# The first load of wq moved ahead of the critical section and cut into 16 and 112 partitions, the store's wait moved into a section of its own, and the order of waits turned round

## The chip, the core and the metric

The kernel runs on one core of one Trainium2 chip. Its time is the device time of one execution in microseconds (us), taken as the median of several runs; lower is better. A profile comes from one more execution, in which every instruction and every DMA packet is recorded. The span in it reaches from the first to the last recorded instruction and is a little shorter than the execution's device time.

## The reference

One token `x` of 576 values is normalised (mean and variance, epsilon 1e-5, no scale or offset) to `xn`. Two branches read `xn`, and the result is their sum with `x`:

```python
q = (xn @ wq)                                   # 576 -> 32 heads x 128
p = softmax(q . k_cache * 128**-0.5)            # k_cache: 32 heads x 16384 keys x 128
A = (p . v_cache) @ wo                          # v_cache likewise; wo: 4096 -> 576
B = (gelu(xn @ w_gate) * (xn @ w_up)) @ w_down  # 576 -> 4608 -> 576, tanh form of gelu
out = x + A + B
```

All of it is float32. One head's keys are 8 MB and its values another 8 MB, so 32 heads read 537 MB; the five weight matrices add some 51 MB.

## The kernel before

The order of all work is written out by hand; there is no planner. The class `Order` (L40 to L114) keeps, for every buffer, a log of who last wrote or read which part, with the semaphore and value that says when. `needs` (L59) turns the operands of a new instruction into a list of (semaphore, value) pairs, in the order in which the log gives them: what the operands read comes first, then what the destination overwrites. `op` (L87) issues compute instructions and `dma` (L103) transfers. Both put the first pair of the list on the instruction itself and a separate wait instruction ahead of it for each of the others. L106 is such a separate wait of a transfer, L107 the transfer itself.

The function `tile_decode_kernel` opens one critical section (L120) and calls `decode` in it. At its entry SP releases the other engines, at its exit all five meet. Everything below happens inside.

Three slots of 64 KB per partition over all 128 partitions hold what is streamed from memory: `slot_a`, `slot_b` and `slot_v` (in the code `sa`, `sb`, `sv`). Nearly all transfers are issued by SP, in the order of the program:

1. L197 loads the first 512 rows of `wq` into `slot_a`: four rows of the matrix on each partition, 16,384 values or 64 KB in one piece, 128 partitions, 8 MB. L198 loads the last 64 rows of `wq` into `slot_b`. Then parts of `w_gate` and `w_up` go into `slot_v` and into the rest of `slot_b`. The three small loads of `x` are issued by ACT.
2. Meanwhile VectorE (DVE) and ScalarE (ACT) normalise `x`; TensorE (PE) spreads it over the partitions; DVE writes the copies that the projections use into `z`. `project` (L245) multiplies with `wq` (called at L258: first the part in `slot_b`, then the four quarters in `slot_a`) and later with `w_gate` and `w_up` in `ffn`.
3. The heads. Keys of head h go to `slot_b` (even h) or `slot_a` (odd h), the values of the head before to `slot_v` (L340, L342). DVE multiplies the whole 128 x 16384 slot of keys by the query and reduces it to 128 x 128 scores (both L185); then come the maximum over partitions by way of PE and DVE (L355, L357), its scaled negative `nb` on ACT, the exponentials `pe` on ACT, and 32 products with the values on PE (L305, a loop in PE's own instructions). The next keys for a slot are issued when DVE has reduced the old ones, the next values when PE has used the old ones.
4. The end: `w_down` and `wo` are loaded, DVE sums 28 rows of `w_down`, PE does the rest, DVE copies the result of 4 x 144 values into `z`, SP stores it (L432), and SP waits for the store to land (L433). The section's exit follows, and then the program's own meeting of engines (L457).

Of the kernel before, what the change touches and what calls it, by code (L numbers as in the profile page):

```python
# [8 lines left out]
F32 = mybir.dt.float32  # L9
# [4 lines left out]
P = 128  # L14
H, SK, DH = 32, 16384, 128
D, DF = 576, 4608
R = SK // P
SUB = 64
DJ = 4
DM = P * DJ  # L20
# [15 lines left out]
SLOT_AT = 27904  # L36
SLOT_B = R * DH * 4


class Order:  # L40
# [46 lines left out]
    def op(self, eng, emit, out, *ins, also=(), signal=None):  # L87
        reads, writes = [a for a in ins if a is not None], [out, *also]
        need = self.needs(eng, reads, writes)
        for sem, value in need[1:]:  # L90
            getattr(self.nc, eng).wait_ge(sem, value)
        i = emit(getattr(self.nc, eng))
        if need:
            i._wait_ge(*need[0])
        value = self.count[eng] + 1
        if signal is None:
            self.count[eng] = value
            i.then_inc(self.sem[eng], 1)
        else:
            i.then_inc(signal, 1)  # L100
        self.note(eng, self.sem[eng], value, reads, writes)

    def dma(self, dst, src, sem, value=16, eng="sync", out=False):  # L103
        need = self.needs(eng, [src] if out else [], [] if out else [dst])
        for s, v in need[1:]:
            getattr(self.nc, eng).wait_ge(s, v)  # L106
        i = getattr(self.nc, eng).dma_start(dst, src)  # L107
        if need:
            i._wait_ge(*need[0])
        i.then_inc(sem, 16)  # L110
        if value and not out:
            self.note("dma", sem, value, [], [dst])


SIZES = {}


@with_exitstack
def kernel(ctx: ExitStack, tc: tile.TileContext, x, k_cache, v_cache, wq, wo, wg, wu, wd, out):
    with tc.tile_critical():  # L120
        decode(tc, x, k_cache, v_cache, wq, wo, wg, wu, wd, out)


def decode(tc, x, k_cache, v_cache, wq, wo, wg, wu, wd, out):
    nc = tc.nc
    o = Order(tc)
    names = iter(range(1000))

    def sem():
        return tc.alloc_semaphore(f"d{next(names)}")  # L130

    def sbuf(name, *shape):
        n = 1
        for s in shape[1:]:
            n *= s
        t = nc.alloc_sbuf_tensor(name, [P, n], F32)
        SIZES[t.name] = n
        return t.ap()[: shape[0]]
# [3 lines left out]
        SIZES[t.name] = 512 * banks  # L142
        return t.ap()

    def slot(name, i):
        t = nc.alloc_sbuf_tensor_at(name, [P, R * DH], F32, offset=SLOT_AT + i * SLOT_B)
        SIZES[t.name] = R * DH
        return t.ap()

    kv = k_cache.rearrange("b h (p n) d -> (b h) p (n d)", p=P)  # L150
    vv = v_cache.rearrange("b h (p n) d -> (b h) p (n d)", p=P)
    xf = x.rearrange("b s d -> (b s) d")
# [1 line left out]
    wmain = {n: w[:DM].rearrange("(p j) f -> p (j f)", j=DJ) for n, w in (("q", wq), ("g", wg), ("u", wu))}  # L154
    wtail = {n: w[DM:].rearrange("d (s f) -> (d s) f", s=2) for n, w in (("q", wq), ("g", wg), ("u", wu))}
    wov = wo.rearrange("(p t) f -> p (t f)", t=WO_T)
    wdv = wd.rearrange("(p t) f -> p (t f)", t=WD_T)

    sa, sb, sv = slot("slot_a", 0), slot("slot_b", 1), slot("slot_v", 2)
    ident, ones = sbuf("ident", P, P), sbuf("ones", P, P)  # L160
    eps_t, par, same, quarter = sbuf("eps_t", P, 1), sbuf("par", P, 2), sbuf("same", P, 32), sbuf("quarter", P, 4)
    x2 = sbuf("x2", P, HALF)
# [21 lines left out]
    def dve(name, out, *ins, **kw):  # L184
        o.op("vector", lambda e: getattr(e, name)(out, *ins, **kw), out, *[a for a in ins if isinstance(a, bass.AP)],  # L185
             *[a for a in kw.values() if isinstance(a, bass.AP)])
# [5 lines left out]
    def load(dst, src, **kw):  # L192
        o.dma(dst, src, sem(), **kw)
        return dst

    ROW3 = 3 * DF
    load(sa, wmain["q"])  # L197
    qt = load(sb[:, ROW3 : ROW3 + QS], wtail["q"])  # L198
    row3, tails, at = {}, {}, 0
    for n in "gu":  # L200
# [132 lines left out]
    for h in range(H):  # L333
        s = h % 2
# [32 lines left out]
    def load_rows(t, at, src, lo, n):  # L367
        load(t[:, at * D : (at + n) * D], src[:, lo * D : (lo + n) * D])
        return [t[:, (at + j) * D : (at + j + 1) * D] for j in range(n)]

    first = load_rows(sb, 0, wdv, 0, WD_A)
# [7 lines left out]
    wo_rows, lo = [], 0  # L379
# [36 lines left out]
    for j, w in enumerate(wo_rows):  # L416
# [4 lines left out]
        if j == WO_T - 4:  # L421
            dve("tensor_add", x2[:64], x2[:64], pairs[1][64:, :HALF])
            dve("tensor_add", x2[:64], x2[:64], pairs[0][:64, :HALF])
            for i, g in enumerate(quart):
                r, lo = 32 * (i // 2), i % 2 * QUART
# [2 lines left out]

    o4 = z[:, P : P + QUART]
    dve("tensor_copy", o4, acc4)  # L430
    s_out = sem()
    o.dma(of.rearrange("o (a f) -> (o a) f", a=4), o4[0:P:32, :], s_out, eng="sync", out=True)  # L432
    nc.sync.wait_ge(s_out, 16)  # L433


# [26 lines left out]
```

## Time and profile before

| what | value |
|---|---|
| runs of the kernel before | 1364.62 us median of 3 (1364.61 to 1365.01) |
| device time of the profiled execution | 1364.62 us |
| its span, first to last instruction | 1362.8 us |
| time outside the span | 1.82 us |
| TensorE clock granted, mean | 0.629 of full speed |

How to read the profile: PE is TensorE's matmul and PEld its weight load, DVE VectorE, ACT ScalarE, POOL GpSimd, SP the engine that issues transfers, SPq its queue. A line of a timeline gives start, duration, engine, program line and operation, and in brackets how long the engine had been idle before and what released it. A view by windows gives the busy time of every engine in a stretch, then the clock of PE, the mean busy share of the core's 16 DMA engines (a packet counts in the stretch in which it begins, so short stretches can show more than 1) and what they moved in GB/s. A transfer is cut into packets, and a packet is done by one DMA engine. The chain of work is followed back from the last instruction to what released it at each step.

### The profile page before, as it was taken

The numbers are of one execution on the slowest core, as the hardware profiler recorded it, in microseconds if no ns is written. First come the engines' busy times: TensorE is split into PE (matmuls) and PEld (weight loads), VectorE is DVE, ScalarE is ACT, GpSimd is POOL, SyncE is SP. The second block draws the span as 40 slices with busy tenths as digits, with TensorE's granted clock in tenths as the row PEclk, the third lists the DMA queues.
The fourth block names the chain that finished last, engine by engine and source line by source line (L and its number), as shares of the span: only waits on it lengthen the run. The fifth ranks groups of instructions, "written<-read, shape, count | busy, mean of one in ns | idle before, by whom it ended". The sixth has DMA issues, their size and how long they took to land.

```text
span 1362.8 us, 6967 instructions
## 1 busy us (share of the span) xinstructions
PE 446.2 (33%) x3012; PEld 161.7 (12%) x3012; DVE 1158.1 (85%) x195; ACT 63.2 (5%) x231; POOL 1.0 (0%) x7
## 2 busy tenths in 40 slices
PE   3431233333322333323223333323223333232237
PEld 1110111110111111101101111101111111011012
DVE  1069999899888888899888888998888888988882
ACT  0000000000000000000000000000000000000000
POOL 0000000000000000000000000000000000000000
PEclk9665666666556666666556666665566666655667
DMA  9999999999999999999999999999999999999998
GB/s 398 449 424 431 437 442 439 429 433 433 433 433 431 435 439 442 431 433 431 433 435 431 435 435 442 433 433 433 433 435 431 431 437 440 437 431 433 432 434 347
DMA packets 11832, 587.73 MB, mean 431 GB/s; under 512 B 1319, under 2 KB 1325, under 8 KB 1710
## 3 DMA queue, kind: packets, MB, share of 16 engines
q1 hardware_dynamic: 11816, 587.60, 99.6%
q8 instruction: 5, 0.08, 0.0%
q14 instruction: 5, 0.04, 0.0%
q10 hardware_dynamic: 6, 0.00, 0.0%
HBM read 587.60 MB, written 0.00 MB: 431 GB/s over the span
## 4 chain that ended last, share of the span: by engine, by line
DMA 49%; DVE 39%; issue 0%; PE 0%
DMA slot_b<-in_A_k_cache_dram 43%; DVE slot_b L185 20%; DVE scores L185 19%; DMA slot_b<-in_B_w_down_dram 3%; DMA slot_b<-in_A_wo_dram 3%; PE pg L182 0%; PE pg L317 0%; DVE z L185 0%; DVE nm L357 0%
## 5 line engine op out<-in xcount | busy, mean ns | idle before, releaser
L305 PE MATMUL po<-slot_v,pe 128*4 128x512 f32 x2048 | 293.0, 736 | 607.0 <-PEq L309 607.0
L185 DVE TENSOR_TENSOR slot_a<-slot_a,qs 128x16384 f32<-128x16384 f32 x16 | 275.6, 17223 | 42.7 <-DMA slot_a<-in_A_k_cache_dram 42.7
L185 DVE TENSOR_TENSOR slot_b<-slot_b,qs 128x16384 f32<-128x16384 f32 (+1 forms) x17 | 275.7, 16218 | 38.6 <-DMA slot_b<-in_A_k_cache_dram 38.6
L185 DVE TENSOR_REDUCE scores<-slot_b 128x128 f32<-128x16384 f32 (+1 forms) x17 | 275.7, 16216 | 0.6
L185 DVE TENSOR_REDUCE scores<-slot_a 128x128 f32<-128x16384 f32 x16 | 275.5, 17220 | 0.6
L305 PEld LDWEIGHTS po<-slot_v,pe 128*4 128x4 f32 x2048 | 56.6, 98 | 816.3 <-issue 816.3
L317 PE MATMUL pg<-ident,pm 128*1 128x128 f32 x32 | 11.9, 372 | 240.3 <-PEq L309 240.3
L185 DVE TENSOR_TENSOR slot_v<-pg,same 128x396 f32<-128x396 f32 (+1 forms) x6 | 3.4, 558 | 70.1 <-PE pg L182 69.8
L190 ACT ACTIVATE z<-po 128x512 f32<-128x512 f32 x33 | 19.7, 596 | 888.8 <-PE po L305 888.8
L305 PE MATMUL pc<-same,z 128*128 128x1 f32 x256 | 59.8, 355 | 0.0
L305 PEld LDWEIGHTS pc<-same,z 128*128 128x128 f32 x256 | 57.1, 328 | 0.5
L317 PEld LDWEIGHTS pg<-ident,pm 128*1 128x1 f32 x32 | 2.5, 79 | 245.5 <-issue 245.5
L357 DVE TENSOR_REDUCE nm<-pg 1x1 f32<-1x128 f32 x32 | 8.9, 279 | 17.8 <-PE pg L317 17.8
L185 DVE SCALAR_TENSOR_TENSOR slot_b<-slot_b,hT 128x576 f32<-128x576 f32 x27 | 22.1, 819 | 0.9
L305 PE MATMUL pg<-nm,ones 1*128 1x1 f32 x64 | 17.7, 343 | 14.8 <-PEq L309 14.8
L305 PEld LDWEIGHTS pg<-nm,ones 1*128 1x128 f32 x64 | 15.9, 306 | 24.2 <-issue 24.2
L190 ACT ACTIVATE nb<-pg 128x1 f32<-128x1 f32 x32 | 5.5, 171 | 235.7 <-PE pg L305 235.7
L305 PE MATMUL pqs<-qcur,ones 1*128 1x128 f32 x64 | 15.4, 321 | 1.4 <-PEq L309 1.4
L182 PE MATMUL pg<-slot_b,z 128*32 128x396 f32 (+1 forms) x72 | 7.7, 594 | 19.1 <-DMA slot_b<-in_B_w_gate_dram 19.1
L190 ACT ACTIVATE pe<-scores,nb 128x128 f32<-128x128 f32 x32 | 12.8, 401 | 2.9
L305 PEld LDWEIGHTS pqs<-qcur,ones 1*128 1x128 f32 x64 | 9.4, 182 | 28.7 <-issue 28.7
L185 DVE TENSOR_TENSOR x<-x,qb 64x288 f32<-64x288 f32 x2 | 0.9, 452 | 11.5 <-PE qb L182 11.4
(75 smaller groups left out, 123.6 us busy)
## 6 DMA issues: line engine op xcount, KB each, us to landing
slot_b<-in_A_k_cache_dram SPq DMA_DIRECT2D x2, 4096.0 KB, 23.9
slot_b<-in_B_w_down_dram SPq DMA_DIRECT2D x1, 8064.0 KB, 42.6
slot_b<-in_B_w_gate_dram SPq DMA_DIRECT2D x1, 6912.0 KB, 55.5
slot_a<-in_B_w_up_dram SPq DMA_DIRECT2D x1, 6912.0 KB, 39.8
slot_a<-in_A_wo_dram SPq DMA_DIRECT2D x1, 3456.0 KB, 41.3
slot_v<-in_B_w_gate_dram SPq DMA_DIRECT2D x1, 2304.0 KB, 29.0
slot_v<-in_B_w_up_dram SPq DMA_DIRECT2D x1, 2304.0 KB, 37.5
slot_a<-in_B_w_down_dram SPq DMA_DIRECT2D x1, 2304.0 KB, 28.5
```

What stands on the lines that cost most here:

```text
L182: o.op("tensor", lambda e: e.matmul(outp, lhsT, rhs, start=start, stop=stop), outp, lhsT, rhs, signal=signal)
L185: o.op("vector", lambda e: getattr(e, name)(out, *ins, **kw), out, *[a for a in ins if isinstance(a, bass.AP)], *[a for a in kw.values() i ...
L190: o.op("scalar", lambda e: e.activation(out, src, func, **kw), out, src, kw.get("bias") if isinstance(kw.get("bias"), bass.AP) else None, ...
L305: i = nc.tensor.matmul(dst, lhs, rhs, start=start, stop=stop)
L317: nc.tensor.transpose(pt[:1, :P], pm, ident).then_inc(o.sem["tensor"], 1)
L357: o.op("vector", lambda e: e.tensor_reduce(nm[:1], pt[:1, :P], axis=AX.X, op=ALU.max, negate=True), nm[:1], pt[:1, :P], signal=s_n)
```

## The change

Four edits:

- The three slots are now allocated in `tile_decode_kernel`, and the first load of `wq` into `slot_a` is issued there by SP, ahead of the critical section, as two transfers: partitions 0 to 15 (1 MB) and partitions 16 to 127 (7 MB). Both signal the semaphore `first`, and inside the section the log is told that `slot_a` is written when `first` has reached 32. A no-op on SP that follows the two transfers, and after it the section's entry no-op, release the other engines.
- The wait for the store to land has left `decode`. It stands alone in a second critical section that follows the first one, on the semaphore `done`. The exit of the first section, where all engines meet, no longer stands behind the landing; the second section's entry and exit are SP's alone, and the other engines only branch past it.
- Both sections name SP as their synchronising engine.
- `op` and `dma` put the last pair of the list on the instruction and the others on separate waits ahead of it.

```diff
-        for sem, value in need[1:]:
+        for sem, value in need[:-1]:
             getattr(self.nc, eng).wait_ge(sem, value)
         i = emit(getattr(self.nc, eng))
         if need:
-            i._wait_ge(*need[0])
+            i._wait_ge(*need[-1])
...
-    with tc.tile_critical():
-        decode(tc, x, k_cache, v_cache, wq, wo, wg, wu, wd, out)
+    nc = tc.nc
+    first, done = tc.alloc_semaphore("first"), tc.alloc_semaphore("done")
+    slots = []
...
+    wqv = wq[:DM].rearrange("(p j) f -> p (j f)", j=DJ)
+    for lo, hi in ((0, 16), (16, P)):
+        i = nc.sync.dma_start(slots[0][lo:hi], wqv[lo:hi]).then_inc(first, 16)
+        tc.no_tile_sem_insts.add(i.ins.name)
+        tc.add_to_no_dep_group("first", i.ins)
+    tc.declare_fence(nc.sync.nop().ins, group="first")
+    with tc.tile_critical(sync_engine=mybir.EngineType.SP):
+        decode(tc, x, k_cache, v_cache, wq, wo, wg, wu, wd, out, slots, first, done)
+    with tc.tile_critical(sync_engine=mybir.EngineType.SP):
+        nc.sync.wait_ge(done, 16)
...
-    load(sa, wmain["q"])
+    o.note("dma", s_first, 32, [], [sa])
...
-    s_out = sem()
     o.dma(of.rearrange("o (a f) -> (o a) f", a=4), o4[0:P:32, :], s_out, eng="sync", out=True)
-    nc.sync.wait_ge(s_out, 16)
```

The same two hunks with `need[:-1]` and `need[-1]` stand in `op` and in `dma`.

More of the change, by code (lines that the diff above doesn't have):

```diff
@@ L104, in dma @@
         need = self.needs(eng, [src] if out else [], [] if out else [dst])
-        for s, v in need[1:]:
+        for s, v in need[:-1]:
             getattr(self.nc, eng).wait_ge(s, v)
@@ L108, in dma @@
         if need:
-            i._wait_ge(*need[0])
+            i._wait_ge(*need[-1])
         i.then_inc(sem, 16)
@@ L119, with decode @@
 def kernel(ctx: ExitStack, tc: tile.TileContext, x, k_cache, v_cache, wq, wo, wg, wu, wd, out):
-    with tc.tile_critical():
-        decode(tc, x, k_cache, v_cache, wq, wo, wg, wu, wd, out)
-def decode(tc, x, k_cache, v_cache, wq, wo, wg, wu, wd, out):
+    nc = tc.nc
+    first, done = tc.alloc_semaphore("first"), tc.alloc_semaphore("done")
+    slots = []
+    for i, name in enumerate(("slot_a", "slot_b", "slot_v")):
+        t = nc.alloc_sbuf_tensor_at(name, [P, R * DH], F32, offset=SLOT_AT + i * SLOT_B)
+        SIZES[t.name] = R * DH
+        slots.append(t.ap())
+    wqv = wq[:DM].rearrange("(p j) f -> p (j f)", j=DJ)
[8 more added lines that the diff above has]
+        nc.sync.wait_ge(done, 16)
+def decode(tc, x, k_cache, v_cache, wq, wo, wg, wu, wd, out, slots, s_first, s_out):
     nc = tc.nc
@@ L143, in psum @@
         return t.ap()
[L145 to L148, printed above, removed]
     kv = k_cache.rearrange("b h (p n) d -> (b h) p (n d)", p=P)
@@ L157, in decode @@
     wdv = wd.rearrange("(p t) f -> p (t f)", t=WD_T)
-    sa, sb, sv = slot("slot_a", 0), slot("slot_b", 1), slot("slot_v", 2)
+    sa, sb, sv = slots
     ident, ones = sbuf("ident", P, P), sbuf("ones", P, P)
```

## Prediction

> **What bounds the kernel now.** I read the head of the page first, then the chain of work, then the rate of the transfers in the middle of the run, then DVE's waits.
>
> ```profile
> span 1362.8 us, 6967 instructions
> ...
> PE 446.2 (33%) x3012; PEld 161.7 (12%) x3012; DVE 1158.1 (85%) x195; ACT 63.2 (5%) x231; POOL 1.0 (0%) x7
> ...
> q1 hardware_dynamic: 11816, 587.60, 99.6%
> ...
> DMA 49%; DVE 39%; issue 0%; PE 0%
> ```
>
> The chain mixes DMA (49%) and DVE (39%), so it doesn't say at once which of the two sets the pace. The queue row does: SP's queue q1 keeps the 16 DMA engines busy for 99.6% of the span, DVE only 85%. What ends DVE's idle time agrees:
>
> ```profile
> DVE slot_a L185 <- DMA slot_a<-in_A_k_cache_dram: 42.7, 14, 3.2
> DVE slot_b L185 <- DMA slot_b<-in_A_k_cache_dram: 38.6, 13, 3.0
> ```
>
> In nearly every head DVE waits about 3 us (42.7/14 and 38.6/13) for keys. The DMA engines have no gap to give back, so a delay of a DMA engine anywhere moves the end by as much, while DVE, ACT and PE have about 3 us to spare in each head. Now the rate:
>
> ```profile
> core 0: us, PE busy (x) PEld busy (x) DVE busy (x) ACT busy (x) POOL busy (x), PEclk, DMA share, GB/s
> 200.00:1200.00 1000.00, 319.91 (x2002) 114.92 (x2002) 908.66 (x105) 48.27 (x182) 0.00 (x0) 0.61 1.00 434
> ...
> slot_v<-in_A_v_cache_dram SPq DMA_DIRECT2D x32, 29.3
> slot_a<-in_A_k_cache_dram SPq DMA_DIRECT2D x16, 42.7
> ...
> slot_a<-in_A_wq_dram SPq DMA_DIRECT2D x1, 22.0
> ```
>
> 434 GB/s over 16 engines is 27.1 GB/s for each. A 64 KB row (65,536 bytes, what one partition of a slot takes) is 65,536 / 27,100 = 2.42 us of one engine, and a full slot of 128 rows, eight to an engine, is 19.3 us. The first load of wq took 22.0 us from issue to landing: about 1 us to the first data, 19.3 us, and a slower start. Keys land 42.7 us and values 29.3 us after their issue, so 23 and 10 us of other work lie ahead of them in the engines' queues: SP is never late.
>
> **The change part by part.**
>
> *Start.* These are the rows of the first microseconds, and of the projection that needs x:
>
> ```profile
> 0.34 0.10 POOL L448 MEMSET const-uint8-127<- 128x1 uint8 x1
> 0.91 0.51 ACTq L107 DMA_DIRECT2D slot_v<-in_A_x_dram  x1
> 0.95 0.34 POOL L207 MEMSET x<- 128x288 f32 x1 [0.51 <-SPq L120]
> 0.96 0.39 SPq L107 DMA_DIRECT2D slot_a<-in_A_wq_dram  x1
> ...
> 1.41 0.41 SPq L107 DMA_DIRECT2D slot_b<-in_A_wq_dram  x1
> ...
> 8.69 0.20 DVE L185 COPY z<-tt 128x64 f32<-128x64 f32 x1
> ...
> 25.48 3.55 PE L182 MATMUL qb<-slot_b,z 128*32 128x512 f32 x16 [17.43 <-DMA slot_b<-in_A_wq_dram]
> ```
>
> POOL's last constant ends at 0.44, SP's first transfer is issued at 0.96. Between them lie the program's first meeting of engines and the section's entry; only the entry is skipped. The gain is between 0 and 0.52 us; I take half, 0.25.
>
> One more transfer costs SP 0.45 us (0.96 to 1.41). Nothing waits for that: the second piece is issued 0.45 us after the first, while an engine is busy with its first row for 2.42 us. If that cover were gone it would cost the 0.45 us. The loads behind it in SP's queue (wq's tail, the gate and up parts) are issued some 0.7 us later than now, behind 19 us of rows.
>
> The other engines are released only after both issues, so ACT's loads of x, the constants and the normalisation start some 0.7 us later (0.9 less 0.25), and x's small packets now find rows of wq ahead of them on their engines. The chain they feed ends with z at 8.89 (8.69 + 0.20), and PE stands idle 17.43 us after its part of it, until wq's tail lands. This hides up to 16.6 us (25.48 less 8.89); a delay by one row, even one of four times the length (9.7 us), fits.
>
> *The split.* This is the largest term and the one that no row shows: every large transfer of the trace goes to all 128 partitions. The 16-row piece gives each of the 16 engines one row, all to neighbouring partitions. If every engine keeps its 27.1 GB/s, the piece takes 2.42 us and nothing is lost. If sixteen neighbours are reached through one path of an engine's width, the rows go one after another: 16 x 2.42 = 38.7 us, a loss of 36.3. If the memory's write side is divided over the partitions as the work is over the engines, an eighth of the partitions has two paths for 16 rows, eight to a path. I take four rows to a path, the middle of 1, 2, 4, 8, 16: each engine's first row takes 4 x 2.42 = 9.68 us instead of 2.42 and loses 7.26 us. All engines lose it, and at 99.6% none can make it up.
>
> [...]
>
> The 112-row piece gives each engine seven rows. Its groups of seven no longer lie on the eights of a full slot, so engines can meet on a path here too. The bounds: no sharing, nothing; all seven rows four to a path, 7 x 7.26 = 50.8 us. It is nearer in shape to the full slot than to the narrow piece, so I put it near the low end: the slowest engine shares with one other during three of its seven rows, 3 x 2.42 = 7.26 us. The end waits for the slowest engine, so its loss counts and not the mean.
>
> *The end.* The last rows are these:
>
> ```profile
> 1359.27 0.31 DVE L185 COPY z<-pg 128x144 f32<-128x144 f32 x1 [3.09 <-PE pg L182]
> 1359.65 0.66 SPq L107 DMA_DIRECT2D out_dram<-z  x1
> ...
> SPq L120 <- DMA out_dram<-z: 1.0, 1, 1.0
> ```
>
> The store's issue ends at 1360.31, SP waits 1.0 us, so it lands near 1361.3, and 1.5 us of meetings follow. In the changed kernel the first section's exit falls into that 1.0 us; behind the landing stand SP's own exit and the program's last meeting. A meeting of all engines with an entry took at most 0.47 us at the start (0.44 to 0.91), so the gain is between 0.47 us and, if a second section brings a meeting of its own behind the landing, a loss of 0.47. As the other engines only branch past it I take a gain of 0.2. If the exit did not fit into the 1.0 us, this gain would be gone.
>
> *Order of waits.* The store waited for DVE by a separate wait and then for ACT; now DVE's wait is on the transfer itself. It was issued 0.07 us after DVE's end (1359.58 to 1359.65): at most 0.07 is gained, I take 0.05. In the heads the order is turned on ACT; nb, for instance, gets its late wait (for PE) as the separate one.
>
> ```profile
> L190 ACT ACTIVATE nb<-pg 128x1 f32<-128x1 f32 x32 | 5.5, 171 | 235.7 <-PE pg L305 235.7
> ```
>
> Queued behind it on ACT are the exponentials, for which PE's products wait. Priced by the same 0.07 either way, that is 32 x 0.07 = 2.2 us in all, hidden behind the 3 us that DVE waits for keys in each head, and behind the 10 us queued ahead of the values. Without that cover it would be 2.2 us.
>
> **Sum**, against the profiled execution: 1362.8 - 0.25 (start) - 0.2 (exit) - 0.05 (store) + 7.26 (16 rows) + 7.26 (112 rows) = 1376.8 of span. Outside the span lie 1364.62 - 1362.8 = 1.82 us; its device time of 1364.62 is also the median. That gives 1378.6 us, 1.0% slower.
>
> **Rivals.**
>
> *No sharing.* An engine writes any partition at its own rate. Then only the small gains stay: 1364.62 - 0.5 = 1364.1. For it: 16 engines at 27.1 GB/s is all the trace ever shows. Against it: it shows this only with rows spread over all partitions. This is the case that isn't slower.
>
> *Only the narrow piece shares.* The 112 rows are spread so that engines don't meet. 1364.1 + 7.26 = 1371.4. For it: seven eighths of the partitions are in reach.
>
> *Sharing throughout.* The 112 rows are dealt out in turn, sixteen neighbours at a time, so that four engines meet on each path in every row: 1364.1 + 7.26 + 50.8 = 1422.2. Against it: full slots show no trace of such dealing, as they run at 434 GB/s.
>
> *The early issue gains more.* The DMA engines start their rows between 1.5 and 2.5 us:
>
> ```profile
> 1.00:1.50 0.50, 0.00 (x0) 0.00 (x0) 0.35 (x3) 0.00 (x0) 0.43 (x3) 1.00 0.00 0
> 1.50:2.00 0.50, 0.00 (x0) 0.00 (x0) 0.44 (x2) 0.01 (x1) 0.29 (x1) 1.00 0.83 267
> 2.00:2.50 0.50, 0.00 (x0) 0.00 (x0) 0.44 (x2) 0.50 (x1) 0.00 (x0) 1.00 4.85 1573
> ```
>
> All the 2 us ahead of them, the store's 0.07, and a meeting of 0.47 at the end would give 2.5 us, so even this stays short of 0.2%; faster by more needs something that I don't see.
>
> **How the numbers follow.** Forecast (sharing in both pieces, 1374 to 1383 as its own range, from one to five shared rows) 0.38; no sharing 0.27; only the narrow piece 0.21; sharing throughout 0.11; faster by more than anything priced here 0.03. 0.2% is 2.7 us, about what a measurement of this kernel can tell from no change. Slower: 0.38 + 0.21 + 0.11 = 0.70; same: 0.27; faster: 0.03. The range goes from 1363.6 (no sharing, with the larger gains of start and end) to 1383 and leaves out the 0.11 and the 0.03.
>
> **What would show it.** The windows of the first 15 us: at 434 GB/s nothing is shared; at a quarter of that until some 11 us the first piece goes four to a path. The landing of wq's tail, which lets PE begin at 25.48: 25 without sharing, 32 with the narrow piece, up to 40 with both. From then on every head should start later by one constant amount, with the same 3 us of waiting on DVE and the same 434 GB/s. The first issue on SP should stand near 0.7, and the last 1.5 us should shrink to about 1.3. I am wrong if wq's tail lands as before, or if the delay grows from head to head: then the waits or SP's queue cost something that I have put at nothing.

## The result and the profile after

The changed kernel takes 1385.05 us (median of 6 runs, 1384.23 to 1385.9) against 1364.64 us before (median of 6): a ratio of 1.0149, interval 1.0139 to 1.0159. That is 20.4 us slower. The direction was forecast; the size had been put at 14.0 us, and the time lies 2 us above the range. The profiled execution is the fastest of the six, 1384.23 us with a span of 1382.4, so the traces account for 19.6 us.

The head of the page of the changed kernel:

```profile
span 1382.4 us, 6976 instructions
...
PE 450.2 (33%) x3012; PEld 161.8 (12%) x3012; DVE 1158.2 (84%) x195; ACT 63.2 (5%) x231; POOL 1.0 (0%) x7
...
GB/s 213 388 422 438 438 438 429 434 440 431 430 440 430 432 436 436 429 436 440 429 436 440 429 430 440 433 432 436 432 432 438 434 430 436 438 430 433 437 431 348
...
q1 hardware_dynamic: 11832, 587.60, 99.6%
```

The GB/s of the kernel before, in slices of 34.1 us:

```profile
GB/s 398 449 424 431 437 442 439 429 433 433 433 433 431 435 439 442 431 433 431 433 435 431 435 435 442 433 433 433 433 435 431 431 437 440 437 431 433 432 434 347
```

The share of q1 is the same 99.6%: the DMA engines are busy all the time, but the first slice of the span (34.6 us) moves only 213 GB/s and the second 388, against 398 and 449 before. From the third slice on the rates are the old ones. "Busy" here counts a packet from its start to its end, however slowly it goes (the first sixteen rows of wq took 8.5 us in the median, 3.2 in the kernel before); the loss can be seen in the GB/s and not in the share.

The windows over the changed kernel's two loads of wq into `slot_a`, from the first packet to the last, and over the middle of the run:

```profile
1.70:43.10 41.40, 2.45 (x10) 2.36 (x10) 4.89 (x18) 1.58 (x2) 0.77 (x3) 1.00 1.00 218
...
200.00:1200.00 1000.00, 315.59 (x1966) 113.80 (x1958) 911.69 (x105) 48.17 (x182) 0.00 (x0) 0.61 1.00 434
```

The same load in the kernel before, from its first packet to its landing (its last packet ends at 22.6):

```profile
1.90:23.00 21.10, 2.45 (x10) 2.36 (x10) 4.10 (x15) 1.58 (x2) 0.00 (x0) 1.00 1.00 415
```

What took 21.1 us at 415 GB/s now takes 41.4 us at 218: 20.3 us more, which is the whole loss and a little over. The 434 GB/s of the heads are unchanged, and so is the time that DVE waits for keys in them (14 and 13 waits, 3 us each):

```profile
DVE slot_a L195 <- DMA slot_a<-in_A_k_cache_dram: 43.0, 14, 3.4
DVE slot_b L195 <- DMA slot_b<-in_A_k_cache_dram: 38.1, 13, 3.0
```

So the delay arises once, in the first 43 us, and is carried to the end. The start of the changed kernel on its timeline, with the normalisation and the first projection, and behind it the row of the kernel before that first reads x:

```profile
0.74 0.87 SPq L129 DMA_DIRECT2D slot_a<-in_A_wq_dram  x2
1.91 0.53 ACTq L107 DMA_DIRECT2D slot_v<-in_A_x_dram  x1
...
21.42 0.81 DVE L195 BATCH_NORM_STATS2 small<-slot_v 1x6 f32<-1x288 f32 x2 [16.94 <-DMA slot_v<-in_A_x_dram]
...
26.71 0.20 DVE L195 COPY z<-tt 128x64 f32<-128x64 f32 x1
46.62 3.64 PE L192 MATMUL qb<-slot_b,z 128*32 128x512 f32 x16 [20.55 <-DMA slot_b<-in_A_wq_dram]
```

```profile
3.40 0.80 DVE L185 BATCH_NORM_STATS2 small<-slot_v 1x6 f32<-1x288 f32 x2
```

SP issues wq at 0.74 instead of 0.96. x, issued at 1.91, is there only at 21.42, where the kernel before reads it at 3.40 without a wait; yet PE, which begins at 46.62, waited last for wq's tail (20.55 us), not for x. The last rows:

```profile
1378.95 0.31 DVE L195 COPY z<-pg 128x144 f32<-128x144 f32 x1 [2.93 <-PE pg L192]
1379.29 0.66 SPq L107 DMA_DIRECT2D out_dram<-z  x1
```

The store follows DVE's end (1379.26) after 0.03 us instead of 0.07, and the span ends 3.14 us after DVE's end instead of 3.22 (1362.8 less 1359.58).

### The profile page after: what moved, and what is told of

It is laid out like the page before. It is cut to its first block, busy times and chain, and to the rows that moved or that the text cites. A ratio compares the mean times of both kernels' runs of the same rounds, so it can differ in the third digit from the quotient of the medians.

```text
span 1382.4 us, 6976 instructions
## 1 busy us (share of the span) xinstructions
PE 450.2 (33%) x3012; PEld 161.8 (12%) x3012; DVE 1158.2 (84%) x195; ACT 63.2 (5%) x231; POOL 1.0 (0%) x7
## 3 DMA queue, kind: packets, MB, share of 16 engines
q1 hardware_dynamic: 11832, 587.60, 99.6%
## 4 chain that ended last, share of the span: by engine, by line
DMA 46%; DVE 36%; issue 0%; PE 0%; DVEq 0%
DMA slot_b<-in_A_k_cache_dram 40%; DVE slot_b L195 18%; DVE scores L195 17%; DMA slot_b<-in_B_w_down_dram 3%; DMA slot_b<-in_A_wo_dram 3%; PE pg L192 0%; PE pg L327 0%; DVE z L195 0%; DVEq L91 0%; DVE nm L367 0%
## 5 line engine op out<-in xcount | busy, mean ns | idle before, releaser
L200 ACT ACTIVATE nb<-pg 128x1 f32<-128x1 f32 x32 | 5.5, 171 | 238.0 <-PE pg L315 238.0
L192 PE MATMUL pg<-slot_b,z 128*32 128x396 f32 (+1 forms) x72 | 7.9, 601 | 16.6 <-DMA slot_b<-in_B_w_gate_dram 16.6
## 6 DMA issues: line engine op xcount, KB each, us to landing
slot_a<-in_A_wo_dram SPq DMA_DIRECT2D x1, 3456.0 KB, 41.3
```

Of the source, the lines that this page charges most:

```text
L192: o.op("tensor", lambda e: e.matmul(outp, lhsT, rhs, start=start, stop=stop), outp, lhsT, rhs, signal=signal)
L200: o.op("scalar", lambda e: e.activation(out, src, func, **kw), out, src, kw.get("bias") if isinstance(kw.get("bias"), bass.AP) else None, ...
```

## The experiments

Theory P: the two transfers to part of the partitions are slow by themselves, because rows written beside one another into neighbouring partitions share write paths. Its rivals: the early place costs (E), the source collides (S), the number of rows or of transfers counts (N, Q, W).

**Undo the split alone (e1), do the split alone (e2).**

```diff
 e1, on the changed kernel
-    for lo, hi in ((0, 16), (16, P)):
+    for lo, hi in ((0, P),):
...
-    o.note("dma", s_first, 32, [], [sa])
+    o.note("dma", s_first, 16, [], [sa])

 e2, on the kernel before
-    load(sa, wmain["q"])
+    for lo, hi in ((0, 16), (16, P)):
+        load(sa[lo:hi], wmain["q"][lo:hi])
```

> The changed kernel with its early load of wq as one transfer to all 128 partitions; all else of the change is kept. Theory P (the two narrow transfers are slow, whatever else the change does): the 20.4 us go away and the three small gains are left, 1364.64 - 0.5 = 1364.1 us, between 1363.6 and 1364.6. Rival E (the early place is what costs: x is loaded behind wq, the other engines start late): still slower than before, near 1385.

> The kernel before with its first load of wq cut into 16 and 112 partitions at its old place, inside the section. Theory P: the whole loss appears, and the 0.5 us of small gains are missing: 1385.05 + 0.5 = 1385.5 us, between 1384 and 1387. Rival E: 1364.6 us, as the place is the old one.

e1 took 1364.37 us (11 runs, 1364.15 to 1364.58) against 1364.70, ratio 0.9997, interval 0.9988 to 1.0006. e2 took 1385.30 us, ratio 1.0152, interval 1.0136 to 1.0167. The split is the whole of the loss, at the old place as at the new one, and the early place costs nothing. E falls.

**Destination or source (m1).** Seven transfers of 1 MB, one at a time, ahead of all other large ones:

```diff
+    k0 = kv[0]
+    probe(sb[0:16], k0[0:16])
+    probe(sb[0:16], k0[0:16])
+    probe(sb[0:64:4], k0[0:16])
+    probe(sb[0:128:8], k0[0:16])
+    probe(sb[0:16], k0[0:128:8])
+    probe(sb[0:128:8], k0[0:128:8])
+    probe(sb[:, :2048], k0[:, :2048])
     load(sa, wmain["q"])
```

`probe` issues the transfer and lets SP wait for it.

> The kernel before with seven extra transfers of 1 MB ahead of its first load, each waited for on SP before the next: 16 rows of 64 KB from 1 MB of keys in one piece to neighbouring partitions 0 to 15 (twice); the same rows to every fourth partition from 0 to 60; the same rows to every eighth from 0 to 120; 16 rows from every eighth partition's keys to partitions 0 to 15; those rows to every eighth partition; and 128 rows of 8 KB to all partitions. Its data are overwritten later. An undisturbed row takes 2.42 us, and near 2 us of issue and landing come on top of each transfer. Theory P (destination partitions share paths): rows of 9.7 us to neighbours from either source; to spread partitions well below that, 2.4 to 4.9 us, from either source. Rival S (sixteen engines read one MB at a time and collide at the source): 9.7 us from the one-piece source to any partitions, 2.4 us from the spread source to any partitions. Rival N (any transfer that isn't of 128 partitions is slow): near 9.7 us for the first six alike. [...]

The windows of m1, one for each transfer from its first packet to its last; the second number is the length, the last the GB/s:

```profile
1.90:11.40 9.50, 2.45 (x10) 2.37 (x10) 4.10 (x15) 1.58 (x2) 0.00 (x0) 1.00 0.89 111
13.60:23.20 9.60, 0.00 (x0) 0.00 (x0) 0.00 (x0) 0.00 (x0) 0.00 (x0) 1.00 0.90 109
25.80:31.30 5.50, 0.00 (x0) 0.00 (x0) 0.00 (x0) 0.00 (x0) 0.00 (x0) 1.00 0.82 191
33.20:38.80 5.60, 0.00 (x0) 0.00 (x0) 0.00 (x0) 0.00 (x0) 0.00 (x0) 1.00 0.85 187
40.40:49.80 9.40, 0.00 (x0) 0.00 (x0) 0.00 (x0) 0.00 (x0) 0.00 (x0) 1.00 0.91 112
52.30:58.00 5.70, 0.00 (x0) 0.00 (x0) 0.00 (x0) 0.00 (x0) 0.00 (x0) 1.00 0.86 184
59.70:63.30 3.60, 0.00 (x0) 0.00 (x0) 0.00 (x0) 0.00 (x0) 0.00 (x0) 1.00 0.82 291
```

Neighbours take 9.4 to 9.6 us from either source; the same rows to spread partitions take 5.5 to 5.7 us from either source; the same megabyte over all partitions takes 3.6. For 16 rows the destination decides; S and N fall. The 16-row piece thus loses 9.5 - 3.6 = 5.9 us.

**Shapes, with rows of 16 KB (m2).** The same kind of kernel for nine destinations, 16 KB of each partition (those left out are 0 to 111, 0 to 63, 0 to 31 and 32 to 127):

```diff
+    probe(sb[0:128, :4096], k0[0:128, :4096])
+    probe(sb[16:128, :4096], k0[16:128, :4096])
...
+    probe(sb[0:128:2, :4096], k0[0:128:2, :4096])
+    probe(sb[0:8, :4096], k0[0:8, :4096])
+    probe(sb[0:4, :4096], k0[0:4, :4096])
     load(sa, wmain["q"])
```

> The kernel before with nine extra transfers of 16 KB a partition ahead of its first load, each waited for on SP before the next: partitions 0 to 127, 16 to 127, 0 to 111, 0 to 63, 0 to 31, 32 to 127, the even ones from 0 to 126, 0 to 7, 0 to 3. A 16 KB row takes 0.61 us at 27.1 GB/s, so undisturbed transfers take 4.8, 4.2, 4.2, 2.4, 1.2, 3.6, 2.4, 0.6 and 0.6 us with about 2 us of issue and landing on top of each. Theory P with neighbouring rows to each engine: the 112 rows lose about a fifth more than one row-time (near 5.5 us, as engines meet only now and then), 64 and 32 rows take twice their undisturbed time (4.8 and 2.4), 8 and 4 rows four times theirs (2.4). Rival Q (a transfer off the 128-partition form loses half of the rate whatever its partitions, as the 210 GB/s in the windows from 25 to 40 us of the changed kernel suggest): 8.5 us for 112 rows, wherever they begin, 7.3 for 96, and the even partitions like the 64 neighbours.

The windows of m2, in that order:

```profile
1.90:7.90 6.00, 2.29 (x10) 2.29 (x10) 3.38 (x11) 1.58 (x2) 0.00 (x0) 1.00 0.93 350
9.20:16.10 6.90, 0.00 (x0) 0.00 (x0) 0.00 (x0) 0.00 (x0) 0.00 (x0) 1.00 0.93 266
17.90:24.80 6.90, 0.00 (x0) 0.00 (x0) 0.00 (x0) 0.00 (x0) 0.00 (x0) 1.00 0.92 266
26.70:32.20 5.50, 0.00 (x0) 0.00 (x0) 0.00 (x0) 0.00 (x0) 0.00 (x0) 1.00 0.86 191
34.00:37.10 3.10, 0.00 (x0) 0.00 (x0) 0.00 (x0) 0.00 (x0) 0.00 (x0) 1.00 0.71 169
38.80:46.20 7.40, 0.00 (x0) 0.00 (x0) 0.00 (x0) 0.00 (x0) 0.00 (x0) 1.00 0.93 213
48.30:52.10 3.80, 0.00 (x0) 0.00 (x0) 0.00 (x0) 0.00 (x0) 0.00 (x0) 1.00 0.82 276
53.20:54.90 1.70, 0.00 (x0) 0.00 (x0) 0.00 (x0) 0.00 (x0) 0.00 (x0) 1.00 0.37 77
57.10:58.40 1.30, 0.00 (x0) 0.00 (x0) 0.00 (x0) 0.00 (x0) 0.00 (x0) 1.00 0.20 50
```

Here 112 rows take 6.9 us, longer than the 6.0 us of 128 rows, and no matter where they begin. 64 neighbours go at 191 GB/s, 64 even partitions at 276 in a transfer of only 3.8 us (at 378 with whole rows, in m3): Q falls with that pair and with the 112 rows, for which it had 8.5 us. The 96 rows took 7.4 us, longer than the 112; Q's 7.3 comes close there, and I have no account of them. Two of the expectations missed: I had the 8 and the 4 neighbours at four times their undisturbed time, and these short rows show nothing of it (1.7 and 1.3 us).

**Whole rows, and the two pieces one behind the other (m3).** The list again with rows of 64 KB:

```diff
+    for lo, hi in ((0, 128), (16, 128), (0, 4), (0, 8), (0, 64)):
+        probe((sb[lo:hi], k0[lo:hi]))
+    probe((sb[0:128:2], k0[0:128:2]))
+    probe((sb[0:16], k0[0:16]), (sb[16:128], k0[16:128]))
     load(sa, wmain["q"])
```

In the last probe both transfers are issued before SP waits.

> The kernel before with probes of whole 64 KB rows ahead of its first load, each waited for on SP before the next: partitions 0 to 127, 16 to 127, 0 to 3, 0 to 7, 0 to 63, the even ones, and last 0 to 15 followed at once by 16 to 127, as in the changed kernel. Still open: why the second piece lost some 15 us there, against 7.3 forecast. Theory D (the 112 rows share by themselves): 16 to 127 alone takes 30 us or more against 20.4 for 128 rows. Theory I (the late and uneven start behind the narrow piece sets the engines against each other): 16 to 127 alone scales from its 6.8 us with 16 KB rows to about 24 us, and only the pair takes 40 us and more. For 0 to 3 and 0 to 7: one path for four rows gives near 10 us for each; the 1.15 and 1.63 us of the short rows, had they no such path, give near 3.4. The 64 neighbours should take near 21 us, the even ones near 11.

The windows of m3:

```profile
1.90:23.00 21.10, 2.45 (x10) 2.36 (x10) 4.10 (x15) 1.58 (x2) 0.00 (x0) 1.00 0.96 398
24.30:55.70 31.40, 0.00 (x0) 0.00 (x0) 0.00 (x0) 0.00 (x0) 0.00 (x0) 1.00 0.95 234
57.10:66.10 9.00, 0.00 (x0) 0.00 (x0) 0.00 (x0) 0.00 (x0) 0.00 (x0) 1.00 0.24 29
68.60:77.70 9.10, 0.00 (x0) 0.00 (x0) 0.00 (x0) 0.00 (x0) 0.00 (x0) 1.00 0.46 58
80.10:101.20 21.10, 0.00 (x0) 0.00 (x0) 0.00 (x0) 0.00 (x0) 0.00 (x0) 1.00 0.96 199
102.90:114.00 11.10, 0.00 (x0) 0.00 (x0) 0.00 (x0) 0.00 (x0) 0.00 (x0) 1.00 0.93 378
115.20:156.50 41.30, 0.00 (x0) 0.00 (x0) 0.00 (x0) 0.00 (x0) 0.00 (x0) 1.00 0.95 203
```

The 112 rows alone take 31.4 us where 128 rows take 21.1: theory D holds, and they need no narrow piece ahead of them to be slow. At seven rows to an engine (112 over 16) that is 4.5 us a row; most rows of wq took 2.42 in the trace of the kernel before. The two pieces together take 41.3 us, as in the changed kernel: 20.2 us more than one transfer, 5.9 of them from the first piece and so 14.3 from the second. With whole rows, four neighbours together go hardly faster than the 27.1 GB/s of one engine (9.0 us, 29 GB/s for all four), and eight take hardly longer than four (9.1 us). 64 neighbours need 21.1 us, 64 even partitions 11.1 us for the same bytes.

**The real load cut otherwise (e4, e5, e3, e5b).** All on the kernel before, at the old place:

```diff
-    load(sa, wmain["q"])
 e4 (halves)
+    for lo, hi in ((0, 64), (64, P)):
+        load(sa[lo:hi], wmain["q"][lo:hi])
 e5 (even, odd)
+    for lo in (0, 1):
+        load(sa[lo:P:2], wmain["q"][lo:P:2])
 e3 (columns)
+    for lo, hi in ((0, 2048), (2048, R * DH)):
+        load(sa[:, lo:hi], wmain["q"][:, lo:hi])
 e5b (even, odd, without the log's wait)
+    s_eo = sem()
+    for lo in (0, 1):
+        nc.sync.dma_start(sa[lo:P:2], wmain["q"][lo:P:2]).then_inc(s_eo, 16)
+    o.note("dma", s_eo, 32, [], [sa])
```

> The kernel before with its first load of wq cut into partitions 0 to 63 and 64 to 127, at its old place. Theory P (rows to neighbouring partitions share write paths; 64 neighbours with 16 KB rows moved 1 MB in 5.4 us in the probe, half of the rate of 128 partitions): each half goes at half rate, 2 x 9.7 us are lost, 1364.7 + 19.3 = 1384.0, between 1381 and 1386. Rival W (what costs is a narrow piece, and wider pieces cost less): two pieces four times as wide as the 16 rows lose a few us, 1367 to 1372.

> The same cut into two transfers of 64 rows, but of the even partitions first and of the odd ones then. Theory P: the probe's 64 even partitions took 3.6 us against 5.4 for 64 neighbours, hardly more than undisturbed, so nearly nothing is lost: 1364.7 to 1367. Rival W, or any theory by which the number of rows or of transfers counts: the same time as the halves, which are as many and as wide.

> The kernel before with its first load of wq cut along the rows: 8 KB of each of all 128 partitions first, then the other 56 KB. The first piece has the 1 MB of the 16 partitions, and the transfers are as many. Theory P: all engines keep their rate, and one more issue of 0.45 us is hidden: 1364.7, between 1364.4 and 1365.2. Rival (two transfers in place of one cost, whatever their form): the 20 us of the split.

> The even and the odd partitions again, now issued one behind the other: in the run before SP stood 12.0 us in front of the odd ones until the even ones had landed, as the log takes the two interleaved destinations for overlapping, and the DMA engines stood idle from 13.0 to 14.8 us. Theory P (all of those 3.4 us were that wait and a second slow start): 1364.7, between 1364.4 and 1365.4. If cutting by partitions costs something of its own, near 1368 again.

The halves took 1385.73 us (ratio 1.0154, interval 1.0137 to 1.0171), the columns 1364.55 us (0.9999, 0.9990 to 1.0009), each against 1364.71. e5 took 1368.07 us (1.0024, 1.0015 to 1.0034), more than expected, and its SP queue tells why:

```profile
SPq L107 <- DMA slot_a<-in_A_wq_dram: 12.0, 1, 12.0
```

`Order` describes a destination by its first and last partition, so it takes the odd partitions for an overlap of the even ones, and SP waited for them to land. Without that wait, e5b took 1365.05 us (0.9998, 0.9986 to 1.0010). Its median lies 0.34 us above the other, though the ratio is below 1; one of the 32 runs of the kernel before took 1372.73 us. Two transfers of 64 rows thus cost 21.0 us when they are halves and no more than some 0.3 us, which the interval doesn't tell from nothing, when they interleave. W falls, and so does every theory that counts rows or transfers. That it is the destination which slows the pieces of 64 and 112 rows is carried over from the 16 rows of m1: with the even and the odd rows the source changes too, so a part of the source in these wide pieces isn't excluded.

**The small gains (s1, s2, e6).** s1 is the kernel before with one early transfer to 128 partitions and nothing else of the change, s2 the kernel before with the second section and nothing else. e6 is the changed kernel with its early load cut along the rows:

```diff
-    for lo, hi in ((0, 16), (16, P)):
-        i = nc.sync.dma_start(slots[0][lo:hi], wqv[lo:hi]).then_inc(first, 16)
+    for lo, hi in ((0, 2048), (2048, R * DH)):
+        i = nc.sync.dma_start(slots[0][:, lo:hi], wqv[:, lo:hi]).then_inc(first, 16)
```

> The kernel before with its first load, as one transfer to 128 partitions, issued ahead of the section, and nothing else. In the trace of the changed kernel the first issue stands at 0.74 against 0.96, so I expect 0.22 us less: 1364.5 against 1364.7. If the later release of the other engines or x behind wq cost anything at the end, no gain or a loss.

> The kernel before with the store's wait in a second section and both sections' engine named, and nothing else. In the traces DVE's last copy ends 3.22 us before the span's end in the kernel before, and 3.06 us in the changed kernel with one early transfer (1362.32 against 1359.26): 0.1 to 0.2 us less, 1364.55 against 1364.7. If the second section brings a meeting of engines of its own, 1365.2.

> The changed kernel with its early load cut along the rows, 8 KB of each of all 128 partitions first and then 56 KB. Theory P: nothing of the 20 us, 1364.3, like the one early transfer (1364.37). If a short first piece lets the engines start sooner, up to 0.3 us less than that, 1364.1.

Against 1364.71 us, s1 took 1364.45 us (0.9998, 0.9989 to 1.0007), s2 1364.67 us (0.9999, 0.9990 to 1.0009) and e6 1364.25 us (0.9997, 0.9987 to 1.0006; 11 runs, 1364.04 to 1364.40). The medians stand in the expected order, but every interval takes in 1. e6 is the lowest time of all; that it beats the kernel before by 0.46 us is likely from the runs, whose ranges don't meet (1364.46 is the lowest of the kernel before), and not shown by the interval.

## Why the prediction was wrong

- **DMA bounds all of it; a delay goes to the end undiminished.** Right. The 20.3 us lost in the first 43 us are in the end time, and the heads run as before.
- **Start, 0.25 us gained.** Right as far as can be told: the first issue moved by 0.22 us, and s1's median by 0.26, which is within its interval. The other engines start 1.0 us later (ACT's first load at 1.91 against 0.91), not 0.7.
- **The later x is hidden.** Right in the result, wrong in the working. I had priced a delay of one long row, 9.7 us, under a cover of 16.6; z was finished 18.0 us later (26.91 against 8.89), more than the old cover. By the packets in the trace x waited for three rows and not for one: its 2,304 bytes start at 15.77, when two slow sets of rows (8.5 and 5.3 us in the median) have gone, and the four-byte packet that follows them at 20.61, after a third (4.7 us). In the kernel before, x's packet starts at 1.80, ahead of the first row of wq at 1.98. The delay stayed hidden because wq's tail came 21 us later too. In e1, where wq is fast, DVE had x at 10.18 against 3.40 or earlier, still within the cover.
- **16 rows, 7.26 us.** Nearly right, a little large: 5.9 us. In m3 four neighbours move 29 GB/s together, as if they shared one path of an engine's 27.1. The four was the middle of a list, though, and no row of the trace before spoke for it, so that it holds is in part luck. What I left out is that an undisturbed first row isn't 2.42 us: the first sixteen rows of wq took 3.2 us in the median in the kernel before, and 8.5 in the changed one, which is 5.3 us more.
- **112 rows, 7.26 us: this step failed.** The prediction said: "It is nearer in shape to the full slot than to the narrow piece, so I put it near the low end: the slowest engine shares with one other during three of its seven rows". The runs show 14.3 us, as much as if nearly every row shared with one other and not three in seven. In the changed kernel's trace the rows of the second piece, taken sixteen at a time in order of start, took 5.3, 4.7, 3.0, 3.7, 4.5, 4.6 and 4.4 us in the median, where the kernel before has 2.42 each time: no set is undisturbed, and together they are 13.2 us over. So PE, which was to begin at 40 at the latest, began at 46.62. I had judged the piece by its width, seven eighths of all partitions, and width isn't what counts (m3): 64 interleaved partitions load at 378 GB/s and 112 adjoining ones at 234. How the engines' sevens lie on the partitions, and by what path a row is written, the traces don't show, so why so many rows are slowed, and the third set less than the others, is left open.
- **The end, 0.2 us, and the store's wait, 0.05 us.** The store's wait gave 0.04 us; both together 0.08 (3.22 to 3.14 us), less than the 0.25 that I took. s2 alone, 0.04 us, can't be told from nothing.
- **Order of waits, nothing.** Right. ACT's idle time ahead of nb is 238.0 us against 235.7, but 235.0 to 237.4 in experiments that keep the old order, so no price can be read from it.
- **The sum.** With the measured terms it is -0.22 - 0.08 + 5.9 + 14.3 = 19.9 us, against 19.6 between the spans; the 14.3 is what m3's pair lost less the 5.9. The median of the runs is 0.8 us above the profiled one: three of the six lie between 1384.2 and 1384.5, three between 1385.6 and 1385.9, and the trace doesn't explain what parts them.
- **The rivals.** No sharing and sharing in the narrow piece alone are refuted by m1 and m3, sharing four to a path throughout by m3 (41.3 us, not 79). The forecast's own case came true with one term half its size, and the upper end of the range, drawn at five shared rows, was too low by a row.

## What to carry to other kernels

A DMA engine that shows as busy may run at half rate, as here with 218 GB/s against 415, so read GB/s in the stretch of the transfer and not the busy share alone. Cut a transfer along its rows and keep all 128 partitions in each piece, which cost nothing here (1364.55 us against 1364.71); a cut by partitions was as cheap only into the even and the odd ones (1365.05, the halves 1385.73), and there the dependency log must not take them for overlapping (1368.07). Spreading alone isn't enough: 16 rows over every fourth or eighth partition still took 5.5 us and more, against 3.6 for the same megabyte over all. In this kernel, whose DMA engines never rest (99.6%), what was lost at the start was paid at the end: 20.3 us in the first 43 us, 19.6 us between the spans.

## What the runs showed of the hardware that was not expected

- A transfer of fewer rows can take longer than the full one: 112 rows of 64 KB took 31.4 us, 128 rows 21.1, and 64 adjoining rows as long as 128.
- A few short rows don't show the slowing: four neighbouring partitions took 9.0 us for 64 KB each, but 1.3 us for 16 KB each, a seventh of the time for a quarter of the bytes. With 64 rows of 16 KB it does show (5.5 us for neighbours, 3.8 for even partitions).
- x's 2 KB load, on ACT's own queue, waited from 1.91 to about 21.4 us behind slow rows of wq; in the kernel before it was issued at 0.91 and there by 3.40.
